# Infini-attention and Fourier mixing on one core: the folds of both Fourier layers issued in another order

## The chip, the cores and the metric

The kernel is one program on one core of a Trainium2 chip. The metric is the device time of one execution in microseconds (us); several executions give a median. One further execution was taken with the hardware profiler, and every duration below is from that one. Engines are named as in the profile: PE is TensorE (PEld its weight loads), DVE is VectorE, ACT is ScalarE, POOL is GpSimd, SP is the queue that issues nearly all DMAs.

## The reference, cut to what matters

Four residual layers on x of 2048 rows by 512 columns, in float32: Fourier mixing, attention, Fourier mixing, attention.

```python
def _A_ref(x, dft_seq_re, dft_seq_im, dft_hid_re, dft_hid_im):
    a = jnp.einsum("bsd,ed->bse", x, dft_hid_re)
    b = jnp.einsum("bsd,ed->bse", x, dft_hid_im)
    return jnp.einsum("ts,bse->bte", dft_seq_re, a) - jnp.einsum("ts,bse->bte", dft_seq_im, b)

x = x + _A_ref(_layernorm(x), ...)      # layer 1
x = x + _B_ref(_layernorm(x), ...)      # layer 2: 32 heads of 16, 4 segments of 512 rows, causal softmax
x = x + _A_ref(_layernorm(x), ...)      # layer 3   plus a memory that is carried over the segments
x = x + _B_ref(_layernorm(x), ...)      # layer 4
```

## The kernel before

**A Fourier layer by folds.** The rows of a Fourier matrix repeat with signs, so the 2048 rows are cut into eight octants of 256 rows, and rows that meet the same coefficient are added or subtracted first ("folded"). `OCTANTS` pairs the octants into A, B, C and D. For each half k (0 and 1: 128 rows of every octant) there is one tile of 128 x 2 x 512 for each of A, B, C and D; in the trace A and B are hAB, C is hC, D is hD. First every row is normalised (`normalise`, L364 to L384): `bn_stats` (L369) and `bn_aggr` (L370) of each 128 x 512 tile on DVE, a power on POOL (L374) with a Newton step of five small DVE operations (L375 to L379), then the normalisation itself on ACT (L384) or DVE (L382). Then the folds on DVE, each over 128 x 1024: D01 = A - C and D32 = B - D (both named hD in the trace), S01 = A + C and S32 = B + D (hS), all at L387. `fold_odd` (L389 to L399) makes from D01 and D32 the operands re and im of the odd products, written over A and B. `fold_even` (L401 to L418) makes from S01 and S32 the operands of the even products, in two steps: sums over 128 x 1024 into C and D (L404, L405), then four results of 128 x 512, "two" and "zero", into hS (L408 to L412), with two rows of one partition copied by ACT (L413, L415).

**The products.** `contract(ps)` (L568 on) runs for two halves of the output, ps 0 and 1. For ps 0 its steps are odd and even, for the real (kind 0) and the imaginary part (kind 1), for k 0 and 1. An odd step is eight products of 128 x 256, with an operand of 128 x 128 as weights; an even step is eight of 128 x 128, and for k = 0 also products over one single row (`rows`) and of one single column (`cmid`). Each product stands as two records in the trace, since float32 is passed in two instructions. All PE instructions keep the order in which the program calls them. `drain` takes the results from PSUM, `hidden(j)` does the transform over the 512 columns, adds x and writes the rows to DRAM, and the rows of the first segment go straight into the attention's first normalisation.

**Attention.** Four segments of 512 rows; per segment four groups of eight heads. Projections are products in three parts (hi and lo splits of both operands, `matmul3`). The output projection of the last segment of layer 2 (`outproj`, PE po<-wo,oh) makes four tiles of 128 rows in the order 2, 0, 3, 1 (`ROW_ORDER`). These 512 rows are the octants 6 and 7, that is tile D of layer 3. `take` (L340 on) receives each: the sum with the residual goes to hD (L345), a copy of it to DRAM.

**What sets the order.** The program is a list of generators with time slots (`place`); in each slot they are called in order of a number. A list scheduler then orders each engine's instructions by its own estimates, within priorities (`tc.high_priority`), and every engine runs its list strictly in order. DMAs are nearly all issued by SP, also in order: first the tiles of layer 1, then the coefficients cf, the weights wq, wk and wv, and `chk`, 512 KB blocks of the given Fourier matrices that ACT compares with the expected values (L676) while the Fourier layers run.

**Where the change touches.** `take`, `normalise`, `fold_odd`, `fold_even`, `fold`, `odd`, `contract`, and at the end of the kernel the slots handed to `place_folded`, to the weights and to `setup` (L1354; it makes the identity and other constants, among them `beta_b`, a gate that is loaded by DMA and put through an exponential on ACT, L1389).

## Time and profile before

| | us |
|---|---|
| median of 3 executions | 1302.94 |
| lowest, highest | 1295.02, 1304.22 |
| the profiled execution's own time | 1305.26 |
| its span | 1303.4 |

| engine | busy us | share of the span |
|---|---|---|
| PE | 1158.1 | 89% |
| DVE | 966.3 | 74% |
| ACT | 873.4 | 67% |
| POOL | 462.0 | 35% |

The span runs from the first to the last instruction of the core; 1.9 us of the time lie outside it. A busy share is an average over stages that have different limits, so it says little on one stage. The mean granted clock of PE over the span is 0.944 of full speed. In the views, a row of the timeline gives start, duration, engine, line, operation, output and inputs with their shapes, and how often; where the engine sat idle before it, the idle time and what ended it stand in brackets. Equal neighbours are merged into one row, whose duration is that of all of them.

### The profile page before, as it was taken

The page shows a single profiled execution, that of the slowest core. Times are in us where ns is not written, and L with a number is a line of the kernel's source. Part 1 is how long each engine was busy: PE and PEld are TensorE (multiplying, and loading weights), DVE is VectorE, ACT ScalarE, POOL GpSimd, SP SyncE. Part 2 cuts the span into 40 slices and gives each one's busy share as a digit, 9 for nine tenths or more (in the row PEclk, how much of TensorE's full clock was granted, in tenths as well). Part 3 has the DMA queues.
Part 4 walks back from the last instruction along what each step waited for, and adds up shares of the span by engine and source line. Part 5 has one row for each costly group of instructions (what it writes and reads, how often), then busy time and mean ns, then how long its engine had stood idle before and what let it go on. Part 6 is the DMA issues. An engine that isn't in the chain of part 4 may idle for free. (4 is left out here: it accounts for less than half of the span.)

```text
span 1303.4 us, 24180 instructions
## 1 busy us (share of the span) xinstructions
PE 1158.1 (89%) x7462; PEld 745.5 (57%) x7462; DVE 966.3 (74%) x3511; ACT 873.4 (67%) x1980; POOL 462.0 (35%) x826
## 2 busy tenths in 40 slices
PE   1987897999999999988769878979999999999987
PEld 1875454656565666643358754536565656666544
DVE  8783788778877877787393738877788778777872
ACT  2757376877677777867515553768776777778773
POOL 1110543534444444542300105435344444445431
PEclk9998988999999999998887988979998999999998
DMA  7898643444443443363326886424343434433411
GB/s 275 275 335 303 192 143 106 149 121 126 127 138 100 130 141 105 99 199 112 114 78 245 298 257 197 129 84 152 118 128 126 137 101 130 140 106 99 139 59 52
DMA packets 111093, 197.64 MB, mean 152 GB/s; under 512 B 13885, under 2 KB 63043, under 8 KB 110954
## 3 DMA queue, kind: packets, MB, share of 16 engines
q1 hardware_dynamic: 107690, 195.22, 46.3%
q8 instruction: 61, 1.00, 0.3%
q10 hardware_dynamic: 3264, 0.79, 0.3%
q14 instruction: 78, 0.64, 0.2%
HBM read 128.04 MB, written 67.14 MB: 150 GB/s over the span
## 5 line engine op out<-in xcount | busy, mean ns | idle before, releaser
L868 DVE CUSTOM_DVE_ANT_0 junk<-nat,mask 128x512 bf16<-128x512 f32 (+3 forms) x1024 | 500.2, 488 | 148.8 <-PE nat L85 117.1
L934 ACT ACTIVATE pT<-sT 128x512 f32<-128x512 f32 x640 | 370.5, 597 | 24.2 <-PE pv_bank L85 6.8
L937 POOL TENSOR_SCALAR_AFFINE_SELECT pT<-pT 128x256 f32<-128x256 f32 (+1 forms) x448 | 194.4, 447 | 447.7 <-ACT pT L934 407.6
L85 PE MATMUL nat<-stkk,stkq 96*128 96x512 bf16 (+3 forms) x1024 | 243.7, 310 | 39.0 <-DVE mx L868 16.8
L85 PE MATMUL sT<-stkq,stkk 99*128 99x256 bf16 (+3 forms) x1024 | 251.9, 311 | 26.4 <-DVE mx L868 13.4
L933 ACT ACTIVATE sT<-sT 128x256 f32<-128x256 f32 (+1 forms) x640 | 208.6, 334 | 74.9 <-PE sT L85 69.1
L85 PEld LDWEIGHTS <-stkk 99*128 99x128 bf16 x1024 | 83.8, 100 | 154.1 <-issue 125.3
L85 PE MATMUL pv_bank<-pT,vt 128*17 128x512 f32 (+3 forms) x2048 | 161.7, 455 | 1.9 <-POOL pT L937 1.9
L85 PEld LDWEIGHTS <-stkq 96*128 96x128 bf16 x1024 | 94.6, 101 | 90.2 <-issue 50.8
L85 PE MATMUL pqk<-xT,wq 128*128 128x512 f32 x384 | 132.2, 460 | 8.0 <-DVE xT L99 4.1
L85 PE MATMUL pqk<-xT,wk 128*128 128x512 f32 x384 | 129.3, 449 | 0.0
L85 PE MATMUL po<-wo,oh 128*128 128x512 f32 x384 | 125.1, 446 | 3.7 <-DVE oh L99 2.8
L85 PE MATMUL pvv<-wv,xT 128*128 128x512 f32 x384 | 122.3, 432 | 2.8 <-DVE mx L868 2.8
L676 ACT ACTIVATE chk<-chk,reps 128x1024 f32<-128x1024 f32 (+1 forms) x80 | 81.2, 1018 | 61.1 <-DMA chk<-in_chk 59.1
L85 PEld LDWEIGHTS pv_bank<-pT,vt 128*17 128x17 f32 x2048 | 55.2, 100 | 92.1 <-issue 85.1
L85 PE MATMUL u<-cf,hAB 128*128 128x256 f32 x256 | 66.0, 417 | 34.5 <-DVE hAB L393 24.0
L1005 ACT ACTIVATE ot<-pv_bank 128x512 f32<-128x512 f32 x64 | 38.3, 598 | 75.1 <-PE pv_bank L85 75.1
L85 PEld LDWEIGHTS pqk<-xT,wq 128*128 128x128 f32 x384 | 73.5, 202 | 20.8 <-DVE xT L99 5.3
L868 DVE DVE_READ_ACCUMULATOR2_ANT mx<- 128x1 f32 x1024 | 84.2, 82 | 0.0
L85 PEld LDWEIGHTS po<-wo,oh 128*128 128x128 f32 x384 | 70.7, 198 | 23.0 <-DVE oh L99 6.0
L808 POOL TENSOR_TENSOR parts<-rem,parts 128x512 bf16<-128x512 f32 x60 | 70.9, 1182 | 28.9 <-ACT parts L804 27.6
L85 PEld LDWEIGHTS pqk<-xT,wk 128*128 128x128 f32 x384 | 70.9, 200 | 13.3 <-issue 2.5
(197 smaller groups left out, 1662.5 us busy)
## 6 DMA issues: line engine op xcount, KB each, us to landing
chk<-in_chk SPq DMA_DIRECT2D x68, 512.0 KB
stkq<-scrq SPq DMA_DIRECT2D x64, 384.0 KB
stkk<-scrk SPq DMA_DIRECT2D x64, 384.0 KB
scrq<-parts SPq DMA_DIRECT2D x32, 384.0 KB
scrk<-parts SPq DMA_DIRECT2D x32, 384.0 KB
mid<-xrm SPq DMA_DIRECT2D x32, 256.0 KB
scrq<-parts SPq DMA_DIRECT2D x32, 256.0 KB
scrk<-parts SPq DMA_DIRECT2D x32, 256.0 KB
```

The lines of the kernel that those rows point to most:

```text
L85: return tc.keep_in_program_order(op(*args, **kwargs))
L676: A.activation(t[:, c : c + row], t[:, c : c + row], AF.Abs, bias=rep[:, col : col + 1], scale=scale, accum_out=acc[:, col : col + 1],)
L808: E.tensor_tensor(out=parts[:, 2], in0=rem, in1=parts[:, 1], op=ALU.subtract)
L868: V.tensor_tensor_reduce(junk[:, :n], src, mask[:, 512 - n :], 1.0, 3e38, ALU.add, ALU.min, dst,)
L933: A.activation(blocks, blocks, AF.Relu)
L934: A.activation(dst, ps, AF.Exp, scale=-SCALE)
L937: G.affine_select(blocks, blocks, pattern=[[0, n] for n in blocks.shape[1:-1]] + [[1, P]], compare_op=ALU.is_ge, fill=0.0, base=0, channel ...
L1005: A.activation(ot, pb, AF.Copy)
```

## The change

In layer 1, a new generator `open_folds` takes the place of `fold`. All DVE instructions in it keep the order in which they are written. For half 0 the statistics of D come after the scale of A and C is known, and B and D are normalised by DVE alone; the odd folds are written before anything of half 1, and the sum S01 and `fold_even(0)` only after the statistics of half 1. The statistics of A and C of half 1 are made by ACT (`bn_on_a`: two passes over each tile with a running sum, and two operations on one column). PE gets one product that waits for the scale of A and C, and 52 products of the identity with itself, whose result is not used. The re operand has a tile of its own. In layer 3, `take` makes the statistics of each of the last four tiles as it arrives (rows that belong to another tile have their statistics copied), and `take_in` normalises and folds each tile for itself; the odd products start with that part of the operand. The weights wq and wk are loaded in later slots, and their splits on DVE stand behind the last fold.

```diff
-        split(w[:, 0], w[:, 1], raw)
+        with tc.issue_after(opened[0].ins) if opened else nullcontext():
+            split(w[:, 0], w[:, 1], raw)
...
+            if w == "re" and late is not None:
+                w = "A"
...
+        ENDS = {0: 2, 3: 0}
...
             with tc.high_priority(offset=URGENT):
                 V.tensor_tensor(out=dst, in0=ps, in1=xr, op=ALU.add)
-                if i == 3:
-                    V.tensor_copy(dst[0:1], parts[0][0:1])
-            if i == 3:
-                V.tensor_tensor(out=xo, in0=ps, in1=xr, op=ALU.add)
-            else:
+                bn(mv[:, i], dst)
+                if i != 1:
+                    V.tensor_copy(own[0:1, i], mv[0:1, i])
+                for n, of in (*((n, of) for n, of in ENDS.items() if n == i), *(((2, 3),) if i == 3 else ())):
+                    V.tensor_copy(mv[0:1, n], own[0:1, of])
                 A.activation(xo, dst, AF.Copy)
-            for n, of, r, k in ((0, 2, 1, 0), (3, 3, 0, 1)):
-                if i == n:
-                    A.activation(quad("D", k)[0:1, r], parts[of][0:1], AF.Copy)
+                for n, of, r, k in ((0, 2, 1, 0), (3, 0, 0, 0), (3, 3, 0, 1)):
+                    if i == n:
+                        A.activation(quad("D", k)[0:1, r], parts[of][0:1], AF.Copy)
...
+        def take_in(k, r):
+
+            i = {(6, 0): 0, (6, 1): 1, (7, 1): 2, (7, 0): 3}[OCTANTS["D"][r], k]
+            mv, x_ = row["mv"], quad("D", k)[:, r]
+            rr = sb.tile([P, 1], F32, name="rr", bufs=2)
+            ve, r_, t = (sb.tile([P, 1], F32, name=n, bufs=b) for n, b in (("ve", 3), ("r", 3), ("rt", 2)))
+            V.tensor_scalar_add(ve, mv[:, i, 1:2], EPS)
+            G.tensor_tensor(out=r_, in0=ve, in1=half_neg, op=ALU.pow)
+            V.scalar_tensor_tensor(t, r_, r_, ve, op0=ALU.mult, op1=ALU.mult)
+            V.tensor_scalar(t, t, -0.5, 1.5, op0=ALU.mult, op1=ALU.add)
+            V.tensor_mul(rr, r_, t)
+            V.tensor_scalar(x_, x_, mv[:, i, 0:1], rr, op0=ALU.subtract, op1=ALU.mult)
+            V.tensor_tensor(out=quad("D32", k)[:, r], in0=quad("B", k)[:, r], in1=x_, op=ALU.subtract)
+            fold_re(k, r)
+            V.tensor_tensor(out=quad("S32", k)[:, r], in0=quad("B", k)[:, r], in1=x_, op=ALU.add)
+            fold_im(k, r)
...
+        def bn_on_a(mv, t, junk):
+
+            s_ = sb.tile([P, 2], F32, name="sums2", tag="st", bufs=2)
+            A.activation(junk, t, AF.Copy, accum_out=s_[:, 0:1])
+            A.activation(s_[:, 1:2], s_[:, 0:1], AF.Copy, scale=-1.0 / D)
+            A.activation(junk, t, AF.Square, bias=s_[:, 1:2], accum_out=mv[:, 1:2])
+            A.activation(mv[:, 0:1], s_[:, 0:1], AF.Copy, scale=1.0 / D)
...
+        def warm(gate, n):
+
+            ps = bank("warm")
+            T.matmul(ps[:, : gate.shape[1]], ident, gate, start=True, stop=True)
+            for _ in range(n):
+                T.matmul(ps[:, :P], ident, ident, start=True, stop=True)
...
+            with pinned(mine), tc.high_priority(offset=2 * URGENT):
+                ac, bd = Norm(0, "AC"), Norm(0, "BD")
+                ac.stats()
+                ac.root()
+                bd.stats("B")
+                ac.newton()
+                ac.apply()
+                warm(ac.nb, 52)
+                bd.stats("D")
+                bd.root()
+                bd.newton(on_a=False)
+                bd.apply("BD")
+                odd_folds(0)
+            yield
+            with pinned(mine), tc.high_priority(offset=2 * URGENT):
+                ac, bd = Norm(1, "AC"), Norm(1, "BD")
+                ac.stats(junk=quad("S01", 1)[:, 0])
+                bd.stats()
+                ac.root(1.0 / D)
+                bd.root()
+                half(0, "A", "C", "S01", ALU.add)
+                ac.newton()
+                ac.apply()
+                bd.newton()
+                bd.apply()
+                fold_even(0)
+            yield
+            with pinned(mine), tc.high_priority(offset=URGENT):
+                odd_folds(1)
+                half(1, "A", "C", "S01", ALU.add)
+                opened.append(fold_even(1))
+            yield
...
+            half(k, "A", "C", "D01", ALU.subtract)
+            half(k, "A", "C", "S01", ALU.add)
+            yield
+            for r in (1, 0):
+                with tc.high_priority(offset=URGENT):
+                    take_in(k, r)
                 yield
-                yield
-                half(k, "A", "C", "D01", ALU.subtract)
-                yield
-                with tc.high_priority(offset=URGENT):
-                    normalise(k, "D", "D")
-            with tc.high_priority(offset=URGENT) if late is not None else ahead(k):
-                half(k, "B", "D", "D32", ALU.subtract)
-                half(k, "A", "C", "S01", ALU.add)
-                half(k, "B", "D", "S32", ALU.add)
-                fold_odd(k)
...
+            rows_tile()
+            with tc.high_priority(offset=URGENT) if k == 0 else nullcontext():
                 fold_even(k)
...
         def odd(ps, kind, k):
-            for ab in range(2):
+            for n, ab in enumerate((0, 1) if late is None else (1, 0)):
...
-                        quad("AB"[kind], k)[:, ab, d * P : (d + 1) * P],
+                        quad(("re", "B")[kind], k)[:, ab, d * P : (d + 1) * P],
...
-                steps = [(odd, 0, 0), (odd, 1, 0), (even, 0, 0), (even, 1, 0)]
-                steps += [(odd, 0, 1), (even, 0, 1), (odd, 1, 1), (even, 1, 1)]
+                steps = [(f, kind, k) for k in range(2) for f in (odd, even) for kind in range(2)]
...
-            lambda k: [a1 - 12 + 3 * k, a1 - 6 + 4 * k, a1 - 4 + 4 * k, a1 - 2 + 4 * k],
+            [a1 - 12, a1 - 9, a1 - 6, a1 - 3, a1 - 1],
...
-            mids[0], mids[1], b1, ws, lambda k: a1 + 8 + 3 * k // 2 if k < 12 else b1 + 20 + 4 * (k - 12), lambda k: b1 + LB + 8 + k // 2,
+            mids[0], mids[1], b1, ws, lambda k: a1 + 14 + k if k < 12 else b1 + 20 + 4 * (k - 12), lambda k: b1 + LB + 8 + k // 2,
...
-            lambda k: [e - 56 + 6 * k, e - 52 + 6 * k, e - 46 + 6 * k, e - 16 + 14 * k, e - 13 + 13 * k, e - 10 + 13 * k, e + 1 + 4 * k, a2 - 3 + 3 * k, a2 - 1 + 3 * k],
+            lambda k: [e - 56 + 6 * k, e - 52 + 6 * k, e - 46 + 6 * k, e - 16 + 14 * k, e - 13 + 13 * k, e - 10 + 13 * k, e + 1 + 4 * k, *((e + 11, e + 13, e + 14) if k == 0 else (e + 15, e + 15, e + 17))],
...
-        setup_at = 4
+        setup_at = [a1 - 12, a1 + 4]
...
-    place(5, setup(), [setup_at])
+    place(1, setup(), setup_at)
```

What it moves on DVE in layer 1, half 0, before: the folds from D01 (first row) to the first result of `fold_even` (last row).

```order
L387 TENSOR_TENSOR hD_148<-hAB,hC 128x1024
L387 TENSOR_TENSOR hD_179<-hAB,hD 128x1024
L387 TENSOR_TENSOR hS_181<-hAB,hC 128x1024
L387 TENSOR_TENSOR hS_183<-hAB,hD 128x1024
L393 SCALAR_TENSOR_TENSOR hAB<-hD_179,edge_81,hD_148 128x512
L404 TENSOR_TENSOR hC<-hS_181,hS_183 128x1024
L405 TENSOR_TENSOR hD<-hS_181,hS_183 128x1024
L394 SCALAR_TENSOR_TENSOR hAB<-hD_148,edge_80,hD_179 128x512
L408 TENSOR_TENSOR hS_181<-hC 128x512
```

And now, from the end of the odd folds on; mv_253 are the statistics of A and C of half 1, which ACT makes, and hS_302 is S01 of half 0.

```order
L85 TENSOR_TENSOR hAB<-hD_242,hD_244 128x512
...
L85 BN_STATS st<-hD 128x6
L85 BN_AGGR mv_259<-st 128x2
L85 TENSOR_SCALAR ve_254<-mv_253 128x4
L85 TENSOR_SCALAR ve_260<-mv_259 128x4
L85 TENSOR_TENSOR hS_302<-hAB,hC 128x1024
...
L85 SCALAR_TENSOR_TENSOR nb_264<-mv_259,rr_263 128x4
L85 TENSOR_TENSOR hC<-hS_302,hS_249 128x1024
L85 TENSOR_TENSOR hD<-hS_302,hS_249 128x1024
L85 TENSOR_TENSOR hS_302<-hC 128x512
```

The re operand comes directly behind D01 and D32, and S01 with all that follows from it has moved behind the statistics and both Newton steps of half 1.

On ACT in layer 1, before: from the normalisation of half 0 to that of half 1.

```order
L384 ACTIVATE hD<-hD,nb_167,rr_166 128x512
L1389 ACTIVATE beta_b<-beta_b 128x32
L415 ACTIVATE rows<-hC 1x512
L97 ACTIVATE wq<-raw 128x512 x3
L413 ACTIVATE hS_181<-hD 1x512
L97 ACTIVATE wq<-raw 128x512
L384 ACTIVATE hAB<-hAB,nb_214,rr_213 128x512 x2
```

And now, the same stretch; hS_302<-hD (L484) is the one-row copy that was L413.

```order
L444 ACTIVATE hC<-hC,nb_136,rr_135 128x512 x2
L1516 ACTIVATE beta_b<-beta_b 128x32
L400 ACTIVATE hS_265,sums_266<-hAB 128x512
...
L402 ACTIVATE hS_265,mv_253<-hC,sums_281 128x512
L101 ACTIVATE wq<-raw 128x512 x4
L444 ACTIVATE hAB<-hAB,nb_258,rr_257 128x512 x2
L444 ACTIVATE hC<-hC,nb_258,rr_257 128x512 x2
L444 ACTIVATE hAB<-hAB,nb_264,rr_263 128x512 x2
L444 ACTIVATE hD<-hD,nb_264,rr_263 128x512 x2
L484 ACTIVATE hS_302<-hD 1x512
L486 ACTIVATE rows<-hC 1x512
```

The statistics of half 1 stand behind beta_b, and the one-row copies that the even products need stand behind all eight normalisations of half 1, where they stood ahead of them.

On DVE in layer 3, before: the last of the four taken tiles (L345) and what comes between it and the first re (L393).

```order
L345 TENSOR_TENSOR hD<-po,xr 128x512
L370 BN_AGGR mv_8415<-st 128x2 x2
L369 BN_STATS st<-hD 128x6
L373 TENSOR_SCALAR ve_8422<-mv_8415 128x2
...
L382 TENSOR_SCALAR hD<-hD,mv_8415,rr_8425 128x512 x2
L376 TENSOR_TENSOR rt_8475<-rt_8475,ve_8473 128x2
L387 TENSOR_TENSOR hD_8436<-hAB,hD 128x1024
L387 TENSOR_TENSOR hS_8440<-hAB,hD 128x1024
L393 SCALAR_TENSOR_TENSOR hAB<-hD_8436,edge_81,hD_8236 128x512
```

And now; L357 takes the last tile, L463 makes the first re, L461 the second.

```order
L357 TENSOR_TENSOR hD<-po,xr 128x512
L383 TENSOR_SCALAR hD<-hD,mvD,rr 128x512
L380 SCALAR_TENSOR_TENSOR rt<-r,ve 128x1
L384 TENSOR_TENSOR hD_8455<-hAB,hD 128x512
L386 TENSOR_TENSOR hS_8458<-hAB,hD 128x512
L463 TENSOR_TENSOR hAB<-hD_8301,hD_8455 128x512
...
L384 TENSOR_TENSOR hD_8455<-hAB,hD 128x512
L386 TENSOR_TENSOR hS_8458<-hAB,hD 128x512
L461 SCALAR_TENSOR_TENSOR hAB<-hD_8455,edge_81,hD_8301 128x512
```

Behind the last taken tile stand one normalisation and three folds of 128 x 512 until the first re is there; before, it was the rest of the statistics, two normalisations, two folds of 128 x 1024 and re.

## Rows read from the trace of the kernel before

**Rows 1.** Waits of PE up to 130 us: total, times, longest.

```profile
PE u L85 <- DVE hAB L393: 24.0, 1, 24.0
PE nat L85 <- DMA stkk<-scrk: 6.6, 1, 6.6
...
PE pqk L85 <- ACT xT L97: 2.2, 1, 2.2
```

**Rows 2.** Timeline of PE in layer 1.

```profile
24.02 3.78 PE L85 MATMUL u<-cf,hAB 128*128 128x256 f32 x8 [24.02 <-DVE hAB L393]
30.09 6.96 PE L85 MATMUL u<-cf,hAB 128*128 128x256 f32 x24 [2.28 <-DVE hAB L395]
36.89 1.28 PE L85 MATMUL u<-cf,hS 128*128 128x128 f32 x10
...
45.27 3.72 PE L85 MATMUL u<-cf,hAB 128*128 128x256 f32 x16
48.95 2.36 PE L85 MATMUL u<-cf,hS 128*128 128x128 f32 x16
```

**Rows 3.** Timeline of DVE and POOL in layer 1.

```profile
7.09 0.69 DVE L369 BATCH_NORM_STATS2 st<-hC 128x6 f32<-128x512 f32 x1
7.92 0.66 DVE L369 BATCH_NORM_STATS2 st<-hAB 128x6 f32<-128x512 f32 x1
8.74 1.03 POOL L374 TENSOR_TENSOR r<-ve,half_neg 128x4 f32<-128x4 f32 x1 [6.91 <-DVE ve L373]
11.78 0.20 DVE L379 SCALAR_TENSOR_TENSOR nb<-mv,rr 128x4 f32<-128x4 f32 x1
13.71 1.00 DVE L382 TENSOR_SCALAR hAB<-hAB,mv,rr 128x512 f32<-128x512 f32 x2
18.69 1.21 DVE L387 TENSOR_TENSOR hD<-hAB,hC 128x1024 f32<-128x1024 f32 x1
20.95 1.22 DVE L387 TENSOR_TENSOR hS<-hAB,hC 128x1024 f32<-128x1024 f32 x1
23.22 0.74 DVE L393 SCALAR_TENSOR_TENSOR hAB<-hD,edge,hD 128x512 f32<-128x512 f32 x1
```

**Rows 4.** Timeline of ACT in layer 1.

```profile
12.02 1.52 ACT L384 ACTIVATE hAB<-hAB,nb,rr 128x512 f32<-128x512 f32 x2 [7.17 <-DVE nb L379]
19.41 0.23 ACT L1389 ACTIVATE beta_b<-beta_b 128x32 f32<-128x32 f32 x1 [3.06 <-DMA beta_b<-in_beta]
```

**Rows 5.** Groups of ACT by shape up to 130 us: busy us, mean ns.

```profile
L676 ACT ACTIVATE chk<-chk,reps 128x1024 f32<-128x1024 f32 x32 | 36.6, 1146 | 21.2 <-DMA chk<-in_chk 19.6 <-DVE sums L685 1.2 <-ACT chk L676 0.3
L676 ACT ACTIVATION_READ_ACCUMULATOR chk<-chk,reps 128x1 f32 x40 | 7.6, 189 | 0.0
...
L676 ACT ACTIVATE chk<-chk,reps 128x256 f32<-128x256 f32 x8 | 4.0, 497 | 2.5 <-DMA chk<-in_chk 2.5
```

**Rows 6.** Stretches: length, busy PE, PEld, DVE, ACT, POOL (instructions), PE clock, DMA.

```profile
24.00:28.00 4.00, 3.78 (x8) 2.52 (x8) 4.00 (x5) 2.65 (x5) 0.00 (x0) 1.00 0.72 281
...
124.00:128.00 4.00, 1.93 (x7) 1.25 (x7) 0.81 (x3) 2.01 (x9) 0.00 (x0) 0.50 1.02 345
```

**Rows 7.** Timeline of PE at the start of layer 3.

```profile
653.32 8.64 PE L85 MATMUL po<-wo,oh 128*128 128x512 f32 x36
670.18 9.47 PE L85 MATMUL u<-cf,hAB 128*128 128x256 f32 x32 [8.22 <-issue]
...
682.93 0.49 PE L85 MATMUL u<-cf,hS 128*128 128x128 f32 x2 [2.39 <-DVE hS L411]
...
694.61 5.77 PE L85 MATMUL u<-cf,hAB 128*128 128x256 f32 x16
700.22 1.95 PE L85 MATMUL u<-cf,hS 128*128 128x128 f32 x16
```

**Rows 8.** A stretch of layer 3, columns as in rows 6.

```profile
692.00:696.00 4.00, 4.00 (x14) 3.70 (x15) 0.00 (x0) 1.59 (x4) 0.00 (x0) 0.50 0.98 384
```

**Rows 9.** Timeline of DVE and POOL at the start of layer 3.

```profile
659.19 0.69 DVE L345 TENSOR_TENSOR hD<-po,xr 128x512 f32<-128x512 f32 x1 [0.98 <-PE po L85]
...
662.04 0.68 DVE L345 TENSOR_TENSOR hD<-po,xr 128x512 f32<-128x512 f32 x1
...
663.75 0.70 POOL L374 TENSOR_TENSOR r<-ve,half_neg 128x2 f32<-128x2 f32 x1 [12.13 <-DVE ve L373]
...
669.34 0.74 DVE L393 SCALAR_TENSOR_TENSOR hAB<-hD,edge,hD 128x512 f32<-128x512 f32 x1
```

More of the change, by code (lines that the diff above doesn't have):

```diff
@@ L1 @@
 import itertools
-from contextlib import ExitStack, nullcontext
+from contextlib import ExitStack, contextmanager, nullcontext
 from types import SimpleNamespace
@@ L322, in quad @@
             if (w, k) not in h:
-                tag = "ut" if w in ("C", "D32") else "wd"
+                tag = "ut" if w in ("C", "D32", "re") else "wd"
                 h[w, k] = pair(f"h{w}", tag, 8, F32)
@@ L397, in fold_odd, with fold_im @@
             else:
                 V.tensor_tensor(out=re, in0=d, in1=e, op=ALU.subtract)
+        def fold_im(k, r):
+            d, e, im = quad("D01", k)[:, r], quad("D32", k)[:, r], quad("B", k)[:, r]
+            if (k, r) == (0, 0):
+                V.scalar_tensor_tensor(im, d, rest, e, op0=ALU.mult, op1=ALU.add)
+            else:
                 V.tensor_tensor(out=im, in0=d, in1=e, op=ALU.add)
@@ new lines, in fold_even, with open_folds, odd_folds @@
+                return V.tensor_tensor(out=e[:, two], in0=ia, in1=ib, op=ALU.add)
+        def warm(gate, n):
[3 more added lines that the diff above has]
+                T.matmul(ps[:, :P], ident, ident, start=True, stop=True)
+        def open_folds():
+            mine = SimpleNamespace(**{n: in_order(nc.vector, n) for n in VECTOR})
+            def odd_folds(k):
+                half(k, "A", "C", "D01", ALU.subtract)
+                half(k, "B", "D", "D32", ALU.subtract)
+                for r in range(2):
+                    fold_re(k, r)
+                half(k, "B", "D", "S32", ALU.add)
+                for r in range(2):
+                    fold_im(k, r)
+            for w in "ACBD":
+                load(w, 0)
+            yield
+            for w in "ACBD":
+                load(w, 1)
+            yield
[30 more added lines that the diff above has]
+                opened.append(fold_even(1))
+            yield
@@ new lines, in pinned @@
+        @contextmanager
+        def pinned(engine):
+            nonlocal V
+            old, V = V, engine
+            yield
+            V = old
+        def fold(k):
+            load("A", k)
+            load("B", k)
+            yield
+            edge("A", k)
+            edge("B", k)
+            yield
+            normalise(k, "AB")
+            yield
+            load("C", k)
+            yield
+            edge("C", k)
+            yield
+            normalise(k, "C", "C")
+            yield
+            half(k, "A", "C", "D01", ALU.subtract)
+            half(k, "A", "C", "S01", ALU.add)
+            yield
+            for r in (1, 0):
+                with tc.high_priority(offset=URGENT):
+                    take_in(k, r)
+                yield
+            rows_tile()
+            with tc.high_priority(offset=URGENT) if k == 0 else nullcontext():
@@ L638, in edges @@
             yield
-        for k in range(2):
-            place(3, fold(k), fold_at(k))
+        if late is None:
+            place(3, open_folds(), fold_at)
+        else:
+            for k in range(2):
+                place(3, fold(k), fold_at(k))
         for ps in range(2):
@@ L1368, in setup @@
             )
+        yield
+        with tc.issue_after(first_row[0].ins) if first_row else nullcontext():
             same_head = consts.tile([P, HG], F32, name="same_head")
```

122 lines of the change are left out of this document (63 added, 59 removed).

## Prediction

> **What bounds the kernel now.** I began with the clock and the span: the mean granted clock is 0.944 and 1.9 us of the time lie outside the span, so the time follows the span. The chain that ended last says nothing here: it ends in the last write. PE is busy for 89% of the span, so I asked next what PE waits for [rows 1]. The longest wait in the stretch that the change touches is the first: 24.0 us until the first operand re is written. Two more come before the attention: 6.6 us for the DMA of stkk, 2.2 us for xT.
>
> The timeline of PE shows the places where PE waits for folds. In layer 1 the products start at 24.02, wait 2.28 more for im, and then run without a gap [rows 2]. In layer 3 the output projection ends at 653.32 + 8.64 = 661.96, the first product starts at 670.18 (8.22 idle), and before the even products PE is idle for another 2.39 [rows 7]. Elsewhere the change touches nothing that PE waits for, so I sum these two stretches alone.
>
> The clock matters more than the gaps. A product is two records. At full clock (2.4 GHz) sixteen records take 3.72, so a product takes 0.47; the first four of layer 1 took 3.78, or 0.95 each, which is half speed (1.2 GHz) [rows 2], although the window there shows a granted clock of 1.00 [rows 6]. After the idle 6.6 us for stkk the window shows 0.50 [rows 6], and so does the stretch of layer 3 that follows its two gaps [rows 8]. What half clock costs can be read from two rows. From the first even product to the end of the odd ones of half 1, layer 3 needs 694.61 + 5.77 - 682.93 = 17.45 [rows 7], and layer 1, at full clock, 45.27 + 3.72 - 36.89 = 12.1 [rows 2]. The same products cost 5.3 more.
>
> **Layer 1, half 0: the start comes earlier.** Before, nb is made at 11.78, behind other statistics [rows 3]. Now the Newton step of A and C follows POOL's power (8.74 + 1.03 = 9.77) with B's statistics only: four small operations of 0.20 give 10.7. The statistics of D follow, two at 0.83 [rows 3]: 12.4. Then the power again (1.03) and five small operations: 14.6. Four normalisations on DVE (two took 1.00): 16.5. ACT normalises A and C beside this, four at 0.71 [rows 4] from 10.9, done at 13.8. D01 and D32, each 1.13 apart from the next [rows 3]: 18.8; re 0.74: about 19.6. PE starts 4.4 earlier than 24.02. S32 and both im are ready by 22.5 and hold nobody up. The 53 identity products run from 10.9 while PE would be idle, so they cost nothing where they are. If they raise the clock, sixteen odd products at 0.45 to 0.47 end at 26.9.
>
> **Layer 1, even products: the start comes no earlier.** They need S01 and fold_even(0), and these now stand behind the statistics of half 1. ACT's share of those stands behind beta_b, whose DMA landed at 19.41 after 3.06 of waiting [rows 4]; I find nothing that brings that DMA forward, so everything queued behind it waits, the sums of half 1 first. Per tile: two passes at 0.71 and two operations on one column. No row shows such an operation; the two sizes of chk, 1146 ns for 1024 columns and 497 for 256 [rows 5], extrapolate to 0.28 for one column, and the small DVE operation (0.20) is the lower bound. I take 0.2, near that, so 1.85 a tile: 19.65 + 4 x 1.85 = 27.0. The accumulator reads of 189 ns [rows 5] could add 2 x 4 x 0.19 = 1.5; I keep that for the range. DVE's statistics of D share two buffers with ACT's sums and end about 28.8; then two ve, S01 (1.13), two Newton steps of five operations (2 x 1.0): 32.5; the two sums into C and D (2.26) and the first result: 35.5. ACT meanwhile has eight normalisations from 31.5 at 0.71 = 37.2 ahead of the one-row copy that the even products read; priced as a normalisation, it ends at 37.9. Before, they started at 36.89. So the start is 1.0 later, after 37.9 - 26.9 = 11 us of idle PE. The 4.4 won at the front have become a longer gap in the middle.
>
> What that gap does to the clock is the main choice. The nearest row of a gap is the 6.6 us for stkk, after which 0.50 was granted [rows 1, 6]; the start of the program, where 1.00 is shown but four products ran at half, is the milder bound. I take the first: +5.3. By the second the gap costs four products at 0.95 instead of 0.47, +1.9.
>
> The Trainium skill, "TensorE: Matmul & The Clock Gate", section "Why this matters for your kernels", says that idle gaps between bursts of matmuls send TensorE back to half rate, and advises warming it up. By that rule the identity products warm the odd ones and are undone before the even ones, which gives +5.3; by the 1.00 of [rows 6] alone it would be +1.9. The 0.50 of [rows 6] and [rows 8] agrees with the rule.
>
> Layer 1 is then +1.0 + 5.3 = +6.3. Bounds: above, +1.5 for the accumulator reads and +2.2 if the later weights make PE wait for its first projection as long as it did for xT [rows 1]: +10.0. Below, if beta_b and the sums hold nothing up, the start follows the later of DVE and the copy and could be 1.4 earlier, without half clock: -1.4. The wq and wk splits on DVE stand behind the last fold and are priced at nothing: the even and hidden products cover them, and if that cover is gone, it is the 2.2 just counted. The new order of the steps in `contract` moves the first drain one step later; I price it at nothing, since the next products cover it, and at 1 us at most (a step of eight even records).
>
> **Layer 3.** The four tiles of po end 8.64 / 3 = 2.88 apart: 656.2, 659.1, 662.0. Before, the last was taken at 662.04 to 662.72, the power began at 663.75 (0.70), and re was written from 669.34 to 670.08 [rows 9]: DVE does 5 us of work for both last tiles between. Now the statistics of each earlier tile are done in the 2.88 before the next one. For the tile whose fold comes first they and the power are done by about 661 to 662; after the last take (662.7) stand one normalisation (0.50, rows 3), and D32, S32 and re at 128 x 512, half of 1.13 or a little over, 0.6 each: about 665.9. The first row of the operand feeds PE 4.3 earlier, with 3.9 instead of 8.22 of idle. The last tile still needs statistics (0.69), the power (0.70), Newton (1.0), a normalisation and three folds: its re is there at 670.0, im at 673.1, the even operand at 673.7 and its copied row at 674.4. Sixteen products from 665.9, eight of them held by the second tile and the first few at half, end about 676.5, so the even operand is ready before PE comes to it. No second gap, and full clock: the even steps take 45.27 - 36.89 = 8.4 [rows 2] to 684.9, and the odd ones of half 1 3.72 to 688.6, against 700.38: -11.8. I take -11.5. Bounds: -12.5 if the first products run at full clock too; -11.5 + 5.3 = -6.2 if half clock lasts through the even steps.
>
> **Sum.** +6.3 - 11.5 = -5.2; 1305.26 - 5.2 = 1300.1. The profiled run lies 2.3 above the median of 1302.94, so I forecast 1297.8, say 1298. The ends give -1.4 - 12.5 = -13.9 (1289) and +10.0 - 6.2 = +3.8 (1307).
>
> **Rivals.**
> - *Layer 1 keeps its head start.* If the load of beta_b lands before ACT comes to it, the sums of half 1 end some 3 us earlier and the gap shrinks to where few products run at half: -1.4 + 1.0 = -0.4, with layer 3 at its best -12.5: 1290. For it: ACT is free from 13.8 on. Against: the 3.06 of waiting in [rows 4], on a load whose place among the DMAs has not changed. The page named above would grant its warm-up, as far as products follow each other closely.
> - *Half clock in both layers: slower than before.* The second re comes about 4 us after the first, so the first products of layer 3 stand alone with gaps around them; if that keeps the clock down through the even steps, layer 3 gains 6.2 only. With layer 1 at its upper end: +3.8, 1307. It decides as soon as layer 1 loses more than 6.2. For it: 0.50 in [rows 8]. Against: before, PE was idle twice there.
> - *Layer 3 does not do what it says.* The list scheduler may put the split of the last oh, or statistics of other tiles, ahead of the takes; then the first re gains 3 at most and the gap before the even steps remains: +6.3 - 3.0 = +3.3, 1306. Against: the order behind the last take holds one normalisation and three small folds.
>
> **How the numbers follow.** Forecast 0.52, layer 1 keeps its start 0.28, half clock in both 0.13, no gain in layer 3 0.07. A measurement of this kernel tells about 1%, 13 us, from no change: below 1289.9, or above 1316. Half of the first rival and a little of the forecast lie below: faster 0.20. Of the slower cases hardly any passes 1316: slower 0.06. Same 0.74. The range, 1286 to 1310, takes in both ends of the sum and 3 us on each side, since single runs of this kernel lie up to 8 us from their median.
>
> **What would show it.** Layer 1: first u near 19.6; beta_b ending a wait of ACT near 19.4; even products near 38 after some 11 us of idle, with odd records of half 1 longer than 3.72 per sixteen. Layer 3: first u near 666, no gap before the even steps, the odd ones of half 1 taking 3.7 and not 5.8. The forecast is wrong if the even products of layer 1 start before 35, if a clock of 1.00 follows their gap, or if the first nat of layer 2 or 4 waits for something that it did not wait for before.

## The result, and the profile after

The changed kernel takes 1303.51 us (median of 20, 1299.26 to 1311.61). The kernel before, run beside it 20 times, takes 1299.38 us (1290.45 to 1312.61). The ratio is 1.0046, with an interval of 1.0025 to 1.0066: the change makes the kernel slower by about half a per cent, 4 to 6 us. 1298 with a gain of 5.2 was forecast. The ratios leave out executions more than 1.5% above the fastest of the same kernel (three of these 20 of before reach that, and below two of the twelve without identity products), the medians count all, and theirs is a ratio of 1.0032 here.

The two profiled executions would not tell so: 1304.07 us after against 1305.26 before. The execution of before lies 6 us above the median of its 20. So the traces show where the time moved, and only repeated runs tell the sum.

PE in layer 1 of the changed kernel, by the timeline (start, duration, instructions and count, idle time before and its releaser), to be laid beside [rows 2]:

```profile
11.00 13.83 PE L85 MATMUL warm<-ident 128*128 128x128 f32 x104
24.66 3.62 PE L85 MATMUL u<-cf,hre 128*128 128x256 f32 x16
28.12 3.62 PE L85 MATMUL u<-cf,hAB 128*128 128x256 f32 x16
38.51 2.50 PE L85 MATMUL u<-cf,hS 128*128 128x128 f32 x10 [6.77 <-ACT hS L484]
...
46.01 3.60 PE L85 MATMUL u<-cf,hS 128*128 128x128 f32 x16
...
51.82 5.41 PE L85 MATMUL u<-cf,hre 128*128 128x256 f32 x16
...
72.55 1.50 PE L85 MATMUL yi<-wf,vf 128*128 128x256 f32 x4
```

The identity products end at 24.8, so PE starts on the odd products at 24.66, no earlier than before, though DVE had written the first half of re at 19.2 (18.40 + 0.75, in the rows of DVE below). Then come 6.77 us of idle, and the even products start at 38.51 instead of 36.89. Ten of their records take 2.50, where [rows 2] have 1.28: half clock. The sixteen records at 51.82 take 5.41 where [rows 2] have 3.72: a part of them at half clock.

Why the even products start at 38.51, by the timelines of ACT and DVE:

```profile
19.80 0.23 ACT L1516 ACTIVATE beta_b<-beta_b 128x32 f32<-128x32 f32 x1 [6.40 <-DMA beta_b<-in_beta]
...
37.85 0.61 ACT L484 ACTIVATE hS<-hD 1x512 f32<-1x512 f32 x1
```

```profile
18.40 0.75 DVE L85 SCALAR_TENSOR_TENSOR hre<-hD,edge,hD 128x512 f32<-128x512 f32 x1
...
25.43 0.69 DVE L85 BATCH_NORM_STATS2 st<-hAB 128x6 f32<-128x512 f32 x1 [2.67 <-ACT hS L402]
...
29.08 1.22 DVE L85 TENSOR_TENSOR hS<-hAB,hC 128x1024 f32<-128x1024 f32 x1
...
35.51 0.69 DVE L85 TENSOR_TENSOR hS<-hC 128x512 f32<-128x512 f32 x1
```

ACT waits 6.40 for beta_b with the sums of half 1 behind it. DVE waits 2.67 for the buffers that it shares with these sums, and S01 and the first result of `fold_even` come at 29.08 and 35.51. The last copy that the even products need starts at 37.85, behind eight normalisations.

The four stretches of the program, by windows (length, busy PE, PEld, DVE, ACT and POOL with their instructions, granted clock of PE, DMA): up to the first product of layer 2, to the end of its last output projection, to the first product of layer 4, to the end. Before:

```profile
0.00:126.07 126.07, 88.98 (x436) 71.96 (x437) 87.22 (x195) 70.60 (x122) 15.00 (x46) 0.97 0.83 295
126.07:661.96 535.89, 489.77 (x3294) 299.14 (x3294) 415.23 (x1620) 379.73 (x889) 221.53 (x381) 0.95 0.43 132
661.96:778.97 117.01, 95.02 (x436) 77.74 (x437) 66.61 (x136) 52.73 (x95) 8.70 (x23) 0.85 0.67 231
778.97:1303.40 524.43, 484.36 (x3296) 296.66 (x3296) 397.22 (x1561) 370.29 (x874) 216.82 (x376) 0.95 0.38 120
```

And after:

```profile
0.00:139.85 139.85, 108.75 (x542) 90.57 (x543) 88.59 (x190) 75.90 (x144) 15.62 (x46) 0.88 0.75 266
139.85:671.09 531.24, 485.65 (x3294) 296.90 (x3294) 416.70 (x1632) 380.41 (x891) 223.04 (x382) 0.96 0.42 132
671.09:777.11 106.02, 90.73 (x437) 73.56 (x438) 65.46 (x139) 52.72 (x95) 9.55 (x24) 0.90 0.75 254
777.11:1302.30 525.19, 484.03 (x3296) 295.71 (x3296) 397.68 (x1561) 370.33 (x874) 215.76 (x376) 0.95 0.39 121
```

The first stretch is 13.8 longer, the third 11.0 shorter, and between them 4.7 come back in layer 2, at a clock of 0.96 instead of 0.95. The clock column points to the cause of the first: a stretch's length times what its clock lacks to 1.00 is 3.8 us before (126.07 x 0.03) and 16.8 after (139.85 x 0.12). That product counts idle PE too, so it is an upper estimate of what the clock costs; the count from the timeline, further below, puts some 9 of the 13.8 us down to the clock.

What PE waits for in the first stretch (total, times, longest), beside [rows 1]:

```profile
PE nat L85 <- DMA stkk<-scrk: 7.2, 1, 7.2
PE u L85 <- ACT hS L484: 6.8, 1, 6.8
PE u L85 <- DVE xrm L741: 2.4, 1, 2.4
PE pqk L85 <- ACT xT L101: 2.2, 1, 2.2
```

Two waits are new: 6.8 for the one-row copy, and 2.4 for xrm, a row block that DVE adds up late, behind splits of wk.

Layer 3, beside [rows 7]:

```profile
662.40 8.69 PE L85 MATMUL po<-wo,oh 128*128 128x512 f32 x36
674.50 3.36 PE L85 MATMUL u<-cf,hAB 128*128 128x256 f32 x8 [3.42 <-issue]
678.43 5.45 PE L85 MATMUL u<-cf,hAB 128*128 128x256 f32 x24 [0.57 <-DVE hAB L461]
683.71 1.28 PE L85 MATMUL u<-cf,hS 128*128 128x128 f32 x10
...
692.10 7.17 PE L85 MATMUL u<-cf,hAB 128*128 128x256 f32 x32
```

PE is idle for 3.42 instead of 8.22, the even products come 12.6 us after the end of po instead of 17.5, without a gap, and the odd ones of half 1 run at full clock (32 records in 7.17; 16 took 5.77 before). The last point is not the rule: of the twelve kernels below with the new layer 3 and its thin products (defined below) together, only this one and "old step order" show 7.17 for these records. The ten others, "even folds first" among them, show 8.86, one execution each:

```profile
678.63 8.86 PE L85 MATMUL u<-cf,hAB 128*128 128x256 f32 x32
```

### The profile page after: what moved, and what is told of

Same layout as the page of the kernel before. It is cut to its first block, busy times and chain, and to the rows that moved or that the text cites. A ratio compares the mean times of both kernels' runs of the same rounds, so it can differ in the third digit from the quotient of the medians.

```text
span 1302.3 us, 24433 instructions
## 1 busy us (share of the span) xinstructions
PE 1169.2 (90%) x7568; PEld 756.7 (58%) x7568; DVE 968.4 (74%) x3520; ACT 879.4 (68%) x2004; POOL 464.0 (36%) x828
## 4 chain that ended last, share of the span: by engine, by line
PE 36%; DVE 8%; issue 3%; ACT 3%; DMA 3%; POOL 1%; SPq 0%; ACTq 0%; DVEq 0%; POOLq 0%
PE pv_bank L85 6%; PE pqk L85 5%; PE nat L85 4%; PE sT L85 4%; DVE junk L993 4%; PE u L85 4%; PE po L85 3%; PE pvv L85 3%; ACT pT L1059 1%; PE pM L85 1%; PE pm L85 1%; PE on L85 1%; PE yr L85 1%; DMA stkk<-scrk 1%; ACT sT L1058 1%
## 5 line engine op out<-in xcount | busy, mean ns | idle before, releaser
L1130 ACT ACTIVATE ot<-pv_bank 128x512 f32<-128x512 f32 x64 | 38.2, 598 | 75.5 <-PE pv_bank L85 75.5
L85 PEld LDWEIGHTS pvv<-wv,xT 128*128 128x128 f32 x384 | 67.4, 189 | 15.8 <-DVE mx L993 5.3
```

What stands on the lines that cost most here:

```text
L85: return tc.keep_in_program_order(op(*args, **kwargs))
L1130: A.activation(ot, pb, AF.Copy)
```

## The experiments

Each was timed beside the kernel before: six executions of "layer 1 only", ten of "no thin products", twelve of each other variant. The starts (us) are from one profiled execution each. Thin products are those over one single row (`rows`) and of one single column (`cmid`). The kernel without them leaves out a part of the result, so its time is no gain.

| kernel | median us | ratio to before | even products of layer 1 | first nat of layer 2 | end of po to nat of layer 4 |
|---|---|---|---|---|---|
| before | 1299 to 1301 | | 36.9 | 126.1 | 117.0 |
| changed | 1303.51 | 1.0046 (1.0025 to 1.0066) | 38.5 | 139.9 | 106.0 |
| layer 3 only | 1292.82 | 0.9958 (0.9931 to 0.9986) | 36.6 | 126.9 | 107.9 |
| layer 1 only | 1312.54 | 1.0106 (1.0065 to 1.0146) | 38.2 | 144.1 | 110.7 |
| even folds first | 1292.97 | 0.9960 (0.9932 to 0.9988) | 32.9 | 128.2 | 109.5 |
| 84 identity products | 1297.95 | 0.9992 (0.9963 to 1.0021) | 40.1 | 136.7 | 105.8 |
| old weight slots | 1308.38 | 1.0051 (1.0017 to 1.0086) | 39.8 | 142.1 | 106.2 |
| no identity products | 1306.38 | 1.0026 (0.9988 to 1.0064) | 38.6 | 139.2 | 104.1 |
| no thin products | 1294.01 | 0.9954 (0.9928 to 0.9980) | 38.4 | 131.2 | 106.0 |
| half 1 on DVE | 1295.47 | 0.9945 (0.9915 to 0.9975) | 31.4 | 130.4 | 108.8 |
| old step order | 1302.97 | 1.0039 (1.0006 to 1.0072) | 37.5 | 136.7 | 107.3 |
| thin products spread | 1297.34 | 0.9985 (0.9955 to 1.0015) | 31.2 | 137.1 | 102.2 |
| 30 identity products | 1288.94 | 0.9917 (0.9886 to 0.9948) | 26.7 | 125.2 | 110.4 |
| old layer 1, spread | 1294.39 | 0.9959 (0.9930 to 0.9988) | 38.2 | 138.2 | 104.4 |
| old order and slots | 1291.87 | 0.9949 (0.9923 to 0.9974) | 27.2 | 129.4 | 105.8 |
| identity in layer 3 | 1291.77 | 0.9923 (0.9892 to 0.9955) | 27.1 | 133.7 | 108.2 |

**The two halves of the change apart.** First the new layer 3 with layer 1, weights and setup as before (`fold_first` holds the loads and folds of before); then the new layer 1 with layer 3 as before (`take`, the order of the steps and the slots too).

```diff
-            place(3, open_folds(), fold_at)
+            for k in range(2):
+                place(3, fold_first(k), fold_at(k))
```

> Layer 1 as before, layer 3 as changed. Theory (layer 3 gains what was forecast, layer 1 loses more than that): first nat of layer 2 near 126 as before, from the end of po to the first nat of layer 4 near 106 instead of 117, time 10 to 11 us below before (about 1289, ratio 0.992). Rival (the 11 us of layer 3 in one profile are clock luck): nearer to before, ratio above 0.997.

```diff
-            for r in (1, 0):
-                with tc.high_priority(offset=URGENT):
-                    take_in(k, r)
+            normalise(k, "D", "D")
+            half(k, "B", "D", "D32", ALU.subtract)
+            half(k, "A", "C", "S01", ALU.add)
+            half(k, "B", "D", "S32", ALU.add)
+            fold_odd(k)
```

> Layer 1 as changed, layer 3 as before. Theory: first nat of layer 2 near 139.9 instead of 126.1, time 12 to 14 us above before (ratio 1.010). Rival (the loss lies in the mix of both, or in layer 2): first nat near 139.9 but time less than 8 us above before.

Layer 3 alone gains 5.5 us (ratio 0.9958), layer 1 alone loses 13.8 (1.0106); 8.3 in sum, against 6.0 by the ratio of both together, within the intervals. So both theories were half right: layer 1 loses what the profile showed, layer 3 gains half of what it showed. The kernel with the new layer 1 only shows why, in the window of its third stretch, where the folds are those of before:

```profile
675.43:786.14 110.71, 92.40 (x438) 75.77 (x437) 66.53 (x136) 52.72 (x95) 8.69 (x23) 0.89 0.69 239
```

The same code takes 110.71 at a clock of 0.89 here, and took 117.01 at 0.85 in the profile of before. So about six of the 11.0 us belong to that one execution of before and its lower clock, which fits the 5.5 of the runs.

**The order of the even folds.** S01 and `fold_even(0)` stand ahead of the statistics of half 1:

```diff
                 odd_folds(0)
+                half(0, "A", "C", "S01", ALU.add)
+                fold_even(0)
             yield
...
-                half(0, "A", "C", "S01", ALU.add)
                 ac.newton()
                 ac.apply()
                 bd.newton()
                 bd.apply()
-                fold_even(0)
```

> As changed, but S01 and fold_even(0) stand directly behind the odd folds of half 0, ahead of the statistics of half 1. Theory (the even products wait for S01 and the one-row copy behind half 1, and the idle of 6.8 us then costs the clock): even products follow the odd ones near 32 without a gap, a smaller gap of 2 to 4 comes before the odd ones of half 1 near 43 instead of 51.8, clock near 1.00 from 32 to 43, first nat near 131, time 8 to 9 us below the changed kernel. Rival (the clock falls anyway, by what PE does there): even records as long as in the changed kernel, gain below 4.

```profile
26.00 3.62 PE L85 MATMUL u<-cf,hre 128*128 128x256 f32 x16
...
32.91 1.28 PE L85 MATMUL u<-cf,hS 128*128 128x128 f32 x10
...
42.57 6.49 PE L85 MATMUL u<-cf,hre 128*128 128x256 f32 x16 [1.21 <-DVE hre L85]
48.90 3.62 PE L85 MATMUL u<-cf,hAB 128*128 128x256 f32 x16
```

As expected: no gap before the even products, 1.28 for the first ten, 1.21 of idle before the odd ones of half 1 at 42.57. The ratio falls from 1.0046 to 0.9960, some 11 us, and stands where layer 3 alone stands. With this one order put back, the loss is gone. One thing is not as expected: the odd records at 42.57 take 6.49, most of them at half clock, after hardly any idle.

**The gap filled, and the identity products taken out.** `warm(ac.nb, 52)` becomes 84, and then 0.

> As changed, but 84 identity products instead of 52, so that the odd products end where the even ones can start. Theory: odd products from 31 to 38, even ones at 38.5 as in the changed kernel, but at full clock: 8.4 for them instead of 13.3, first nat 5 to 6 us earlier than 139.9. Rival A (the clock falls by what the even products are, not by the gap): even records of the same length as in the changed kernel, time unchanged. Rival B (identity products delay PE, and that is the loss): 6 to 7 us slower.

> As changed, without the 52 identity products (one gated product stays). Theory (the even products wait for DVE and ACT at 38.5 whatever PE does before): first odd product near 19.7, the even ones still at 38.5 after an idle of 11 us, first nat within 1.5 us of 139.9, ratio to before 1.004 to 1.008. Rival (the identity products hold PE up by 5 us): even products near 33 to 34 and first nat 4 to 5 us earlier.

```profile
33.20 3.62 PE L85 MATMUL u<-cf,hre 128*128 128x256 f32 x16
...
40.11 1.28 PE L85 MATMUL u<-cf,hS 128*128 128x128 f32 x10
...
44.23 3.27 PE L85 MATMUL u<-cf,hS 128*128 128x128 f32 x16
...
50.04 3.72 PE L85 MATMUL u<-cf,hre 128*128 128x256 f32 x16
```

```profile
19.22 5.50 PE L85 MATMUL u<-cf,hre 128*128 128x256 f32 x16 [8.06 <-DVE hre L85]
...
38.64 2.50 PE L85 MATMUL u<-cf,hS 128*128 128x128 f32 x10 [10.46 <-ACT hS L484]
```

With 84, PE starts the odd products 8.5 us later than with 52 and still gains 5.6 us on the median: the even products follow without idle and start at full clock (1.28). That shows the cost of the idle, at equal folds. The clock falls here too, but later, in the even records from 44.23 on (3.27 for sixteen, where "even folds first" has 2.05). Without identity products the odd ones start at 19.22 as forecast, and it helps nobody: the even ones start at 38.64 after 10.46 of idle. The 52 products neither cost nor earn anything that the ratio (1.0026, 0.9988 to 1.0064) could show.

**The thin products.** The clock that falls without idle led to the products over one row and of one column, which stand together in the even steps. They were left out of layer 1's first half, on the kernel with 84.

```diff
-                    if (kind, n, k) == (0, 1, 0):
+                    if (kind, n, k) == (0, 1, 0) and (ps or late is not None):
...
-            if (ps, kind) == (0, 1):
+            if (ps, kind) == (0, 1) and late is not None:
```

> As with 84 identity products, but the products over one row and of one column are left out of layer 1's first half (part of the result is missing). Theory (without a gap the clock still fell, from 44 us on, because of these thin products): granted clock 1.00 from 33 to 60, and the even steps 5 to 6 us shorter by the products left out. Rival (the clock falls some time after a dense burst whatever follows): a window of 0.6 or less shows again between 40 and 55.

The window from 32 to 60, with them and then without them:

```profile
32.00:60.00 28.00, 28.00 (x160) 25.25 (x159) 21.00 (x31) 16.45 (x26) 0.00 (x0) 0.94 0.49 169
```

```profile
32.00:60.00 28.00, 26.14 (x153) 22.75 (x152) 25.73 (x44) 18.44 (x30) 1.68 (x4) 1.00 0.57 202
```

Left out, the clock stays at 1.00 over the whole stretch; with them it is 0.94. The ratio of 0.9954 is no gain, since work is missing. And the windows are one execution each: the mean clock over all executions of the two kernels is much the same (medians 0.950 and 0.949). In the next ones they were spread instead, one behind each odd product of half 1, on "half 1 on DVE" and on the old layer 1 with the new layer 3:

```diff
+                    if k == 1 and thin:
+                        mm(*thin.pop(0))
...
-                        mm(dst, row["x"][:, d * P : (d + 1) * P], row["c", ps])
+                        thin.append((dst, row["x"][:, d * P : (d + 1) * P], row["c", ps]))
```

> As with B and D of half 1 on DVE, but the products over one row and of one column of half 0 no longer stand together: each follows one odd product of half 1, in both layers. Theory (the clock falls in the stretch of thin products): no window below 0.9 from 30 to 60 in layer 1 and between 680 and 700 in layer 3, time 4 to 8 us below the one with B and D on DVE. Rival (it falls after any long burst, or by chance): the clock falls elsewhere in the layer as much, time within 3 us.

> Layer 1 as before and layer 3 as changed, with the thin products spread in both. Theory (thin products together let the clock fall, layer 3 keeps its gain): layer 3 from the end of po to the first nat 100 to 103 instead of 107.9, time 3 to 6 us below the one with layer 3 only (1287 to 1290). Rival: as that one, ratio 0.996.

```profile
44.31 0.67 PE L85 MATMUL u<-cf,hAB 128*128 128x256 f32 x2 [2.41 <-ACT wk L101]
...
46.57 1.22 PE L85 MATMUL u<-cf,hAB 128*128 128x256 f32 x2
...
48.44 1.22 PE L85 MATMUL u<-cf,hAB 128*128 128x256 f32 x2
...
56.20 3.73 PE L85 MATMUL u<-cf,hS 128*128 128x128 f32 x16
...
692.76 0.70 PE L85 MATMUL u<-cf,hAB 128*128 128x256 f32 x2
```

These rows are of "old layer 1, spread", the last one of its layer 3. For layer 1 the theory fell. The two records of an odd product take 0.67 at 44.31 and 1.22 from 46.57 on, and half clock lasts beyond the last mixed product, through the sixteen even records at 56.20 (3.73, where 1.95 is full clock): spreading them makes the low stretch of layer 1 longer. Whether it is they that let the clock fall is not separated there, since PE had been idle just ahead in both kernels (2.41 and 5.68). In layer 3 of the same two executions it came as the theory said: the same mixture, with no idle just ahead, runs at full clock throughout (0.70 at 692.76), and the stretch is shorter (102.2 and 104.4). But the two ratios (0.9985 and 0.9959) show no gain.

**Half 1 made shorter.** beta_b is loaded in a later slot, and DVE instead of ACT normalises B and D of half 1, on the kernel with the even folds first; then with 30 identity products.

```diff
-                bd.newton()
-                bd.apply()
+                bd.newton(on_a=False)
+                bd.apply("BD")
...
-        setup_at = [a1 - 12, a1 + 4]
+        setup_at = [a1 - 12, a1 + 12]
```

> As with the even folds first, and beta_b loaded later, and B and D of half 1 normalised by DVE instead of ACT. Theory (the odd products of half 1 wait for eight normalisations on ACT, the idle of 1.2 us and half clock follow): ACT's sums of half 1 start near 14 to 16 instead of 19.9, re of half 1 by 40, no gap before the odd ones of half 1, 16 records of them in 3.7 instead of 6.5, first nat near 124 to 125 instead of 128.2, time 3 to 4 us below the one with the even folds first (about 1289). Rival (clock falls at the thin even products whatever the gap): odd ones still 5 to 6.5, gain below 2.

> As with B and D of half 1 on DVE, but 30 identity products instead of 52, so that the odd products start when re is ready near 20. Theory (re of half 1 is ready near 41 and sets the end): odd at 20, even at 27.5 waiting a little for S32 and S01, odd ones of half 1 at 41 after an idle of 4 to 6 us and at half clock: first nat within 2 us of 130, nothing gained. Rival (PE's own queue sets it): everything 3 to 4 us earlier.

```profile
19.40 3.62 PE L85 MATMUL u<-cf,hre 128*128 128x256 f32 x16
22.86 3.62 PE L85 MATMUL u<-cf,hAB 128*128 128x256 f32 x16
26.71 1.38 PE L85 MATMUL u<-cf,hS 128*128 128x128 f32 x10 [0.24 <-ACT hS L484]
...
40.06 6.56 PE L85 MATMUL u<-cf,hre 128*128 128x256 f32 x16 [4.79 <-DVE hre L85]
46.46 3.62 PE L85 MATMUL u<-cf,hAB 128*128 128x256 f32 x16
```

The first brought no gap and yet sixteen records of 5.41 at 41.33, as its rival had it, and its ratio (0.9945) does not differ from that of "even folds first" (0.9960). With 30 products PE starts at 19.40, the even ones at 26.71, and the odd ones of half 1 at 40.06 after 4.79 of idle, mostly at half clock, as the theory had it. But the first nat came at 125.2 and not near 130, and the ratio is 0.9917 (0.9886 to 0.9948), 10.8 us faster than before and the best here; against "half 1 on DVE" its interval overlaps, so the step from 52 to 30 alone is not shown.

**Weights and step order.** The slots of the weights, the order of the steps of layer 1, and both (on the one with 30 identity products) were set back to those of before.

```diff
-            mids[0], mids[1], b1, ws, lambda k: a1 + 14 + k if k < 12 else ...
+            mids[0], mids[1], b1, ws, lambda k: a1 + 8 + 3 * k // 2 if k < 12 else ...
...
-                steps = [(f, kind, k) for k in range(2) for f in (odd, even) for kind in range(2)]
+                steps = [(odd, 0, 0), (odd, 1, 0), (even, 0, 0), (even, 1, 0)]
+                steps += [(odd, 0, 1), (even, 0, 1), (odd, 1, 1), (even, 1, 1)]
```

> As changed, but wq, wk and wv are loaded in the slots of before (their splits still behind the last fold). Theory (the 2.4 us that PE waits for xrm are splits of wk that wait for a late load): that wait goes, first projection 2 to 3 us earlier against the first yi than in the changed kernel (36.1 there, 30.6 before), time 2 to 3 us below the changed kernel. Rival (the drains and xrm are late because the clock fell): interval from first yi to first projection unchanged within 1 us.

> As changed, but layer 1 keeps the order of steps of before (its first drain one step earlier). Theory (both drains now stand behind each other and DVE comes late to xrm): from the first yi to the first projection about 31 to 33 instead of 36.1, the 2.4 of waiting for xrm gone, 2 to 3 us below the changed kernel. Rival (the late loads of wk alone): interval unchanged at 36.

> As the one with 30 identity products, with the weight slots and the step order of layer 1 of before together. Theory (the 4 us more from the first yi to the first projection need both the late loads and the later drains): that interval 31 to 32 instead of 34.4, time 2 to 3 us below the one with 30 identity products. Rival (the splits of wk and wv behind the last fold stand ahead of xrm on DVE whenever they are loaded): interval stays at 34 to 36, time unchanged.

From the first yi to the first projection it is 30.6 us before, 36.1 in the changed kernel, and 35.6, 34.8 and 34.0 in these three. None gains. 3.2 of the 36.1 are a second fall of the clock, which these products have in some executions only; the rest of the excess is the wait for xrm and slightly longer ones for xT. With the old slots PE waits 1.5 for mv in place of the 2.4 for xrm; with the old step order alone the 2.4 stay. That DVE's splits behind the last fold cause these waits was not tried by itself: this stays open.

**Identity products in layer 3.** 14 of them ahead of the first odd product there.

```diff
+                if late is not None and (ps, f, kind, k) == (0, odd, 0, 0):
+                    warm(ident[:, :4], 14)
```

> As the one with 30 identity products, with 14 identity products also between the last po and the first odd product of layer 3. Theory (idle PE ahead of the folded products lets the clock fall there too): mean granted clock from the end of po to the first nat of layer 4 above 0.90 instead of 0.87, that stretch 3 to 5 us shorter than 110.4. Rival (the thin products of the layer let it fall whatever comes before): clock as before, stretch 105 to 110 as in the kernels without them.

```profile
672.00:676.00 4.00, 4.00 (x20) 3.51 (x20) 4.00 (x7) 1.26 (x2) 0.00 (x0) 1.00 0.00 0
676.00:680.00 4.00, 4.00 (x25) 3.20 (x24) 4.00 (x13) 0.00 (x0) 0.00 (x0) 1.00 0.45 118
680.00:684.00 4.00, 4.00 (x19) 3.73 (x20) 4.00 (x7) 1.24 (x2) 0.00 (x0) 0.58 0.78 280
```

The idle of 3.4 is filled and the first products run at full clock (1.96 of idle before the second half of the operand stay), but from 680 on, behind the first row products, 0.58 is granted. The stretch is 108.2: the rival held, and the ratio (0.9923, 0.9892 to 0.9955) does not differ from 0.9917.

## Why the prediction was wrong

*The start of layer 1* was right for the folds and wrong for PE: re was written at 19.2 (19.6 forecast), but the 53 identity products, which should "cost nothing where they are", took 13.8 us and ended at 24.8. I had not worked out how long they run, though [rows 7] had a price for records of this size (sixteen in 1.95, so 104 in 12.7). No time hung on it: without them the even products start at 38.6.

*The even products* started at 38.5 (37.9 forecast) by the chain that the text walked: beta_b at 19.8, ACT's sums until 27.2 (27.0), the eight normalisations, the copy. Their gap was 6.8 and not 11, since PE started late, and the clock fell all the same: in all five kernels with 6 to 10.5 us of idle there, ten even records took 2.50. The +1.0 (1.6 measured) and the half clock both came.

*The sum of layer 1*, "+1.0 + 5.3 = +6.3", is the step that failed. It measured +13.8 by the profile and +13.8 by the runs of layer 1 alone (8.4 to 19.0); the upper bound was +10.0. The count by the two timelines: 1.6 for the start, 6.1 from there to the first yi (34.0 instead of 28.0), then 5.5 more to the first projection and 0.6 to the first nat. What failed above all are the terms that were priced at nothing. I had stopped the sum at the end of the odd products of half 1, as if full clock and a caught-up DVE waited there. The clock fell once more (the first yi and yr took 8.4 instead of 5.2 until the next u, +3.2), and the wait for xrm (2.4) came, of which only the upper bound had something (2.2, for "later weights").

The term +5.3 was also read from unequal stretches. The 682.93 of [rows 7] is not the first even product of layer 3; eight records stand ahead of the gap:

```profile
679.49 1.05 PE L85 MATMUL u<-cf,hS 128*128 128x128 f32 x8
```

Counted from the same product in layer 1, about 37.9, the difference is 6.3; the changed kernel lost 6.6 over these steps. And that stretch is not a price of a gap: two records behind the 2.39 of idle take 0.49, full clock, and the 0.50 of [rows 8] comes only later, among the thin products and behind them. So the size was nearly right, but the row did not show the mechanism that it was taken for.

*Layer 3* did in its places what was forecast: 3.4 of idle (3.9), no second gap, first nat 11.0 earlier (11.5). The sum for its start was off (662.7 + 0.5 + 3 x 0.6 is 665.0, not 665.9; re was written 3.3 us after the end of po, which would be 665.3). But "-11.5" is the other step that failed: the runs give 5.5 (1.8 to 9.0). About half of it was the clock of the one execution that I had, and the full clock of the odd products of half 1, on which the sum counted, came in two of twelve kernels only (7.17 against 8.86).

*The rivals.* The second, half clock and slower than before, had the point right, "as soon as layer 1 loses more than 6.2", and nearly the price (+3.8; +4.1 by the medians), though not the whole mechanism: in layer 3 the even steps began at full clock, and the loss of layer 1 went on behind the steps that the rival counts. I gave it 0.13, and the size of a clock term taken from one execution should have made that more. The first rival is contradicted: beta_b held ACT for 6.40. The third is contradicted by the first product of layer 3 at 3.4 us. The time lay within the range, the sign did not: 1303.5 is above the median of 1299.4. That it lies only 5.5 from the 1298 is in part luck: the base, a median of three, was 3.6 too high, and the same sum from 1299.4 gives 1294.2.

The rule of the Trainium skill that was weighed there ("TensorE: Matmul & The Clock Gate", section "Why this matters for your kernels": idle gaps put the clock back) is borne out by these runs: 6.8 us of idle, then a granted clock of 0.50 from 40 to 44; with the gap filled 1.00 in the same window, and 5.6 us won. It is not all that puts the clock back here, as the thin products show.

## What to carry to other kernels

Starting an engine earlier earns nothing if its next operand comes no earlier: the head start becomes a gap, and on PE the gap costs the clock for the work behind it, here some 6 us for a forecast head start of 4.4. Write the operands of the second step ahead of the statistics of the third. And take no clock term from one profiled execution: repeat the run, or price the step with and without it.

## What the runs showed that I had not expected

The clock falls without any idle. With 84 identity products PE never stopped from 11 to 60, and among the thin products its records went to half speed. In the one execution without thin products that did not happen. In layer 3 it happened in ten of twelve kernels. Why not in every execution is open: the profile of before has the same products in layer 1 and no such fall [rows 2], while "layer 3 only", with the same layer 1, took 3.30 for the sixteen even records at 40.70 (2.05 before). That the thin products are the cause is likely and not shown: with them spread, layer 3 kept full clock and layer 1, behind an idle PE, did not.

Most of the spread between executions goes with this clock. "Half 1 on DVE" took from 1284.49 us at a mean clock of 0.951 to 1303.39 at 0.939. On some 1300 us, 0.012 of the clock is 15.6 us, an estimate that counts idle PE too, of the 18.9 between them. Over its twelve executions time and clock have a correlation of -0.91; it is weaker in "old order and slots" (-0.49).
